# Attention visits taken two units at a time from the sixteenth unit on, and VectorE steps placed on other hooks

## The chip, the cores and the metric

The kernel runs on one core of a Trainium2 chip. The metric is the device time of one execution in microseconds (us). TensorE (PE) multiplies, VectorE (DVE) and ScalarE (ACT) read its results out of PSUM, GpSimd (POOL) works between tiles in SBUF, and SyncE (SP) issues nearly all DMAs, in order.

## The reference

A decayed attention without softmax for 4 batches, 8 heads, 576 positions and head width 64, then two feed-forward layers on the 2304 tokens of width 512, all in float32:

```python
scores = scale * np.matmul(q, k.transpose(0, 1, 3, 2))
Dmat = np.where(rel >= 0, gamma[:, None, None] ** rel[None, :, :], 0.0)
x = np.matmul(scores * Dmat, v)                  # heads side by side: 2304 x 512
h = np.maximum(np.maximum(x @ w1, x @ w2), x @ w3) @ w_out      # 512 -> 768 -> 512
g = h @ w_gate                                                  # 512 -> 1536
out = (g * (1.0 / (1.0 + np.exp(-g))) * (h @ w_val)) @ w_out2   # 1536 -> 512
```

## The kernel before, in words

The program order on every engine is written out by hand, so each engine does its instructions in the order in which the code calls them. Only buffers and data make it wait.

**Attention.** Two heads (a pair `pr`) of one half `h` of a batch make a unit: 32 units, each with 288 positions in three chunks of 96. A visit to unit n is four short runs of matmuls: `a_value(n)` (the part from the running states, L285, and the part from the weighted scores, L289, into `o_ps`), `a_state(n + 1)` (L264, into `m_ps`) and `a_score(n + 1)` (L248, into `s`). ACT copies `o_ps` into `xh` (L292), and DVE makes the remainder `xl` (L294), a chain of small state updates `st` (L274) and the weighted scores `pT` (L250). Later in the visit `a_prep(n + 2)` prepares a unit: POOL scales `ks`, and DVE does two transposes and a product (L233, L234, L235; "the transposes" below).

**Slices.** Between the short runs stand slices of the first feed-forward layer (`f_slice`): 12 matmuls of 288 columns (L358) into one of two buffers `ps`. The result is read by ACT for the first of three weights (L362) and by DVE for the other two (`hmax`, L364). The queue `fq` holds them in the order weight by weight, two halves each, so that of six slices in a row two end on ACT and four on DVE. A slice can begin only when the reader of the slice two before it is done. From unit 16 on a visit holds five slices.

**Early steps.** From unit 16 on each call of `share` also takes one or two steps of `early_steps`, which turns 28 weights of the later layers from doubled words into float32 (`f32_steps`): a load of 512 KB issued two weights ahead, two ACT copies (L115, L121), three DVE operations (L123 and L124 as one step, L126), and a store of 256 KB (L462). Nine such steps fall in a visit. SP also issues in that part the loads of `k` and `v` of a later pair (`a_load`, L167) and its eight transposed pieces `qk` (`t_load`, L188), the former in odd visits and the latter in even ones.

**Middle.** The product with `w_out` runs in six stretches `hx` of 384 tokens (L743). After each of the four result blocks `e` of a stretch, `h_split` makes the high and low parts of the next input (ACT L545; POOL or, for two of six, DVE L546), and some steps of `x_first` or `x_second` prepare the sums of the last layer's Strassen-like scheme (ACT L660, DVE L662 and subtractions of 768 columns).

**Last layers.** 36 groups, each of seven products of six matmuls (L817) into `g1`, `g2`, `g3`, with `out2` (L794, read by DVE L799 or ACT L797) between them. `hook()` is called ten times in a group; it takes steps of `w_steps` (operands of the next block, L602 and L628 to L635) or, in the last three groups before the final twelve, steps of `x_last` by the table `XPLAN` (splits L662, subtractions L699). The groups before the final twelve are numbered j = 0 to 23. The first hook stands just ahead of the second product, whose result DVE takes up as `u` (L833); the product two later on `g2` may start only when that is read. The last hook stands at a group's end.

Of the kernel before, what the change touches and what calls it, by code (L numbers as in the profile page):

```python
# [23 lines left out]
P = 128  # L24
# [44 lines left out]
def retention_moe(ctx, tc, consts, q, k, v, w1, w2, w3, w_out, w_gate, w_val, w_out2, out):  # L69
# [15 lines left out]
    psa_cm = tc.tile_pool(name="ps_att", bufs=1, space=PSUM)  # L85
    psa = psa_cm.__enter__()

    cst_a = att.tile([P, O_G], F32, name="cst_a", tag="cst_a", bufs=1)
    cst_g = att.tile([P, NCONST - O_G], F32, name="cst_g", tag="cst_g", bufs=1)
    ident = cst_a[0:CK, O_ID:O_KS]  # L90
# [50 lines left out]


    PT = 12
    units = [(b, h, pr) for b in range(B) for pr in range(NP) for h in range(2)]
    NU = len(units)
    U = {}
# [61 lines left out]
    def a_prep(n):  # L208

        if n >= NU:  # L210
            return
        bind(n)
        b, h, pr = units[n]
        u = U[n]
        nk = NC - h
        u["ks"] = att.tile([CK, NC, 2, D], F32, name="ks", tag="ks", bufs=3)
        sc = ks_t[:, pr].unsqueeze(1).unsqueeze(3).to_broadcast([CK, nk, 2, D])
        pool.tensor_tensor(u["ks"][:, 0:nk], u["k"][:, 0:nk], sc, ALU.mult)  # L218
        kq = att.tile([P, 2, C], F32, name="kq", tag="kq", bufs=3)
        kt, qg = kq[:, 0], kq[:, 1].rearrange("p (c m) -> p c m", c=NC)  # L220
        g = g_t[:, pr].unsqueeze(1).to_broadcast([P, NC, CK])
        if n < PT:
            tp = psa.tile([P, 2, 512], F32, name="tp", tag="tp")
            for c in range(NC):
                pe.transpose(tp[:, 0, c * CK:(c + 1) * CK], u["k"][:, c].rearrange("p h d -> p (h d)"), ident)
            for c in range(NC):
                for e in range(2):
                    pe.matmul(tp[64 * e:64 * e + 64, 1, c * CK:(c + 1) * CK], u["q"][:, c, e],  # L228
                              dia[pr][:, e], start=True, stop=True)
# [24 lines left out]
    def a_state(n):  # L254

        if n >= NU:
            return
        b, h, pr = units[n]
        u = U[n]
        nk = NC - h  # L260
        m = psa.tile([P, NC, D], F32, name="m_ps", tag="m_ps")
        for c in range(nk):
            for e in range(2):
                pe.matmul(m[64 * e:64 * e + 64, c], u["ks"][:, c, e], u["v"][:, c, e], start=True, stop=True)  # L264
        if h == 0:
            st = states[(b, pr)] = att.tile([P, 2 * NC, D], F32, name="st", tag="st", bufs=3)
        else:
            st = states.pop((b, pr))
        for c in range(nk):
            g = h * NC + c  # L270
            if g == 0:
                act.activation(st[:, 1], m[:, c], ACTF.Copy)
            else:
                dve.scalar_tensor_tensor(st[:, g + 1], st[:, g], e_t[:, pr:pr + 1], m[:, c], ALU.mult, ALU.add)  # L274
        u["st"] = st

    def a_value(n):
# [15 lines left out]
        xs[(2 * b + h, pr)] = (xh, xl)  # L293
        return lambda: dve.tensor_tensor(xl, o, f(xh), ALU.subtract)  # L294


    w_in = {}
    win_units = [(fi, wi) for fi in range(F1) for wi in range(3)]
# [71 lines left out]
    def f_some(n):  # L370
        for _ in range(n):
            if fq:
                f_slice(*fq.pop(0))
# [8 lines left out]
    def visit(n, slices, convs):  # L382
        plan = list(conv_plan(convs))
        done = 0

        def share(j):
            nonlocal done
            upto = len(plan) * (j + 1) // (slices + 1)
# [4 lines left out]
            if n >= 16:  # L393
                for _ in range(1 if j % 2 else 2):
                    next(early, None)

        low = a_value(n)
        if slices:
            share(0)
        if n % 2:  # L400
            a_load(n // 2 + 3)
        else:
            t_load(n // 2 + 2)
        if n % (2 * NP) == 2 * NP - 1:
            fq.extend((n // NP - 1 + h, *w) for w in win_units for h in range(2))
        a_state(n + 1)
        low()
        a_score(n + 1)
        for j in range(slices + 1):
            if j == min(2, slices - 1) or not slices:  # L410
                a_prep(n + 2)
            if j or not slices:
                share(j)
            if j < slices:
                f_some(1)

    EARLY = [(fi, wi) for fi in range(F2) for wi in range(3) if wi < 2 or fi < 3 or fi == F2 - 1]
# [74 lines left out]
    a_state(0)  # L492
    a_prep(1)
    spin(1)
    for n in range(NU):
        if n < NP - 1:
            tables(n + 1)
        if 2 <= n < 6:
            win_load(n - 2)
        if n == 5:  # L500
            win_phase(0, 0)
            win_phase(0, 1)
        if n == 9:
            sp.dma_start(out=cst_g, in_=consts[:, O_G:NCONST])
        visit(n, *((0, 0) if n < 5 else (0, 1) if n < 8 else (4, 2) if n < 13 else (4, 3) if n < 14 else (6, 2) if n < 16 else (5, 0)))
# [164 lines left out]
    def x_second(b, r):  # L670

        t1 = raw("t12")
        dve.tensor_tensor(t1, r["B12"], r["B11"], ALU.subtract)
        yield
        t3 = r["B12"]
        dve.tensor_tensor(t3, r["B22"], t3, ALU.subtract)
        yield
        yield from x_split(b, "T1", t1)
        dve.tensor_tensor(t1, r["B22"], t1, ALU.subtract)
        yield  # L680
        yield from x_split(b, "T3", t3)
# [47 lines left out]
    for hx in range(NHX):  # L729
        b, half = divmod(hx, 2)  # L730
        if half == 0:
            r = {}
            if b < NBK - 1:
                x_open(b)
        for e in range(KD):
            ps = ps_mm.tile([P, 512], F32, name="ps2", tag="mm")
            n = 0
            for fi in range(F1):
                wh, wl = wo[fi]
                hh, hl = hsp[(hx, fi)]  # L740
# [20 lines left out]
        for _ in xsteps:  # L761
            pass
        xsteps = (x_second if half else x_first)(b, r) if b < NBK - 1 else iter(())
    for _ in steps:
        pass
    hw_cm.__exit__(None, None, None)
# [36 lines left out]
    def group(fi, b, hook, lastg=False):  # L803
# [75 lines left out]
        if fi % GRP == GRP - 1:  # L879
# [5 lines left out]
    XPLAN = {(0, 3): 1, (0, 5): 1, (0, 6): 1, (0, 7): 1, (0, 9): 1, (0, 10): 1,  # L885
             (1, 1): 1, (1, 2): 1, (1, 3): 1, (1, 4): 1, (1, 5): 1, (1, 7): 1, (1, 9): 1,
             (2, 1): 1, (2, 2): 1, (2, 4): 1, (2, 5): 1, (2, 7): 1}
    steps = iter(())
    for j, (fi, b) in enumerate(seq):
        if j == 0:  # L890
# [12 lines left out]

        def hook():
            beat[0] += 1
            if j < len(seq) - 3:
                for _ in range(pace):
                    next(steps, None)
            else:
                for _ in range(XPLAN.get((j + 3 - len(seq), beat[0]), 0)):  # L910
                    next(xsteps)

        group(fi, b, hook)
    for _ in xsteps:
# [35 lines left out]
```

## Time and profile before

| | |
|---|---|
| time, median of 3 runs | 830.73 us (830.68 to 832.44) |
| the profiled execution's own time | 830.89 us |
| its span, first to last instruction | 829.1 us |
| granted TensorE clock | 1.00, the 2.4 GHz level |
| PE busy | 816.9 us, 99% of the span |
| DVE / ACT / POOL busy | 566.3 / 315.7 / 209.7 us |

A busy time counts overlapping matmuls once, and the span is 1.8 us shorter than the execution's time. An idle time given with an instruction is counted from the end of the instruction before it on that engine.

### The profile page before, as it was taken

How to read it: one execution, taken by the hardware profiler on the slowest of the kernel's cores; microseconds unless marked ns; L12 is line 12 of the kernel's file. 1: busy time of each engine (PE TensorE's matmuls, PEld its weight loads, DVE VectorE, ACT ScalarE, POOL GpSimd, SP SyncE). 2: the span in 40 equal slices, each digit the busy share in tenths (PEclk: the TensorE clock that was granted, in tenths of full speed). 3: DMA queues.
4: the chain of work that ended last, by engine and by line, in shares of the span. 5: the costliest groups of instructions: out<-in, count | busy, mean ns of one | idle time of the engine just before them, and what ended most of it. 6: DMA issues, size and time to landing. Idle time of an engine off the chain costs nothing.

```text
span 829.1 us, 15469 instructions
## 1 busy us (share of the span) xinstructions
PE 816.9 (99%) x5933; PEld 762.7 (92%) x5933; DVE 566.3 (68%) x1007; ACT 315.7 (38%) x633; POOL 209.7 (25%) x194
## 2 busy tenths in 40 slices
PE   9999999999999999999999999999999999999998
PEld 6799999899989999999999999999999899999996
DVE  2678857787764354477387799888889875455554
ACT  3554523324321223555354544344444332332220
POOL 4243420000000002343032233323332233322331
PEclk9999999999999999999999999999999999999999
DMA  9999849999981233866334334443422016665532
GB/s 178 236 217 214 175 113 252 238 250 245 252 231 70 80 100 93 247 178 187 137 124 152 141 140 165 165 146 134 165 77 70 20 51 242 217 227 214 191 104 76
DMA packets 162921, 135.08 MB, mean 163 GB/s; under 512 B 101024, under 2 KB 137632, under 8 KB 162848
## 3 DMA queue, kind: packets, MB, share of 16 engines
q1 hardware_dynamic: 161488, 133.69, 56.0%
q8 instruction: 46, 0.75, 0.4%
q10 hardware_dynamic: 1360, 0.41, 0.2%
q14 instruction: 27, 0.22, 0.1%
HBM read 89.77 MB, written 44.30 MB: 162 GB/s over the span
## 4 chain that ended last, share of the span: by engine, by line
PE 67%; issue 14%; DVE 7%; POOL 6%; DMA 2%; ACT 2%; SPq 1%; POOLq 0%; ACTq 0%; DVEq 0%
PE ps L358 25%; PE g L817 17%; PE ps L794 11%; PE ps L743 6%; POOL gl L865 3%; POOL p L838 2%; PE s L248 2%; PE o_ps L289 2%; PE o_ps L285 2%; DMA w<-in_moe_w_val_dram 1%; PE m_ps L264 1%; SPq L188 1%; PE tp L228 1%; DMA kn<-in_k_dram 1%; PE psz L380 1%
## 5 line engine op out<-in xcount | busy, mean ns | idle before, releaser
L358 PE MATMUL ps<-xl,wh 128*128 128x288 f32 x576 | 173.1, 300 | 3.4 <-DVE hmax L364 2.8
L358 PE MATMUL ps<-xh,wh 128*128 128x288 f32 x576 | 169.7, 295 | 0.0
L358 PE MATMUL ps<-xh,wlo 128*128 128x288 f32 x576 | 169.6, 294 | 0.0
L865 POOL TENSOR_TENSOR gl<-p,gh 128x384 fp32r<-128x384 f32 x72 | 85.5, 1205 | 290.1 <-ACT gh L864 290.1
L794 PE MATMUL ps<-wp,gh 128*128 128x512 f32 (+1 forms) x436 | 135.4, 392 | 0.8 <-DVE acc L799 0.7
L358 PEld LDWEIGHTS ps<-xl,wh 128*128 128x128 f32 x576 | 108.0, 188 | 7.6 <-DVE hmax L364 4.0
L358 PEld LDWEIGHTS ps<-xh,wh 128*128 128x128 f32 x576 | 108.1, 188 | 0.0
L358 PEld LDWEIGHTS ps<-xh,wlo 128*128 128x128 f32 x576 | 108.1, 188 | 0.0
L794 PEld LDWEIGHTS ps<-wp,gh 128*128 128x128 f32 x436 | 80.7, 188 | 15.1 <-DVE acc L799 1.8
L364 DVE TENSOR_TENSOR hmax<-ps,hmax 128x288 f32<-128x288 f32 x96 | 43.5, 455 | 69.0 <-PE ps L358 61.1
L794 PE MATMUL ps<-wp,gl 128*128 128x512 f32 (+1 forms) x218 | 85.6, 393 | 0.0
L799 DVE TENSOR_TENSOR acc<-ps,acc 128x512 f32<-128x512 f32 (+1 forms) x91 | 61.9, 683 | 29.5 <-PE ps L794 28.3
L817 PE MATMUL g<-xhB,wa 128*128 128x384 f32 x288 | 73.4, 336 | 0.0
L817 PE MATMUL g<-xhT,wc 128*128 128x384 f32 x288 | 73.2, 335 | 0.0
L546 POOL TENSOR_TENSOR hl<-hf,hh 128x384 fp32r<-128x384 f32 x26 | 30.0, 1164 | 129.3 <-DMA h_d<-hmax 77.4
L864 ACT ACTIVATE gh<-p 128x384 fp32r<-128x384 f32 x72 | 37.8, 525 | 61.0 <-DVE p L868 53.5
L218 POOL TENSOR_TENSOR ks<-kn,cst_a 96x384 f32<-96x384 f32 (+1 forms) x32 | 26.4, 826 | 126.1 <-PE m_ps L264 107.8
L853 ACT ACTIVATE sb<-u 128x384 f32<-128x384 f32 x36 | 18.9, 525 | 100.0 <-DVE u L851 100.0
L817 PEld LDWEIGHTS g<-xhB,wa 128*128 128x128 f32 x288 | 52.1, 188 | 0.0
L817 PEld LDWEIGHTS g<-xhT,wc 128*128 128x128 f32 x288 | 52.0, 188 | 0.0
L362 ACT ACTIVATE hmax<-ps 128x288 f32<-128x288 f32 x48 | 19.7, 410 | 84.1 <-PE ps L358 83.8
L794 PEld LDWEIGHTS ps<-wp,gl 128*128 128x128 f32 x218 | 40.9, 188 | 9.0
(120 smaller groups left out, 1694.1 us busy)
## 6 DMA issues: line engine op xcount, KB each, us to landing
w<-in_moe_w_out_dram SPq DMA_DIRECT2D x18, 512.0 KB, 4.1
w<-l_d SPq DMA_DIRECT2D x28, 256.0 KB, 3.0
h_d<-hmax SPq DMA_DIRECT2D x48, 144.0 KB, 3.3
w<-in_moe_w_dram SPq DMA_DIRECT2D x12, 512.0 KB, 6.6
w<-in_moe_w_gate_dram SPq DMA_DIRECT2D x12, 512.0 KB, 5.9
w<-in_moe_w_val_dram SPq DMA_DIRECT2D x12, 512.0 KB, 5.9
vn<-in_v_dram SPq DMA_DIRECT2D x16, 288.0 KB, 7.9
out_dram<-acc SPq DMA_DIRECT2D x17, 256.0 KB, 2.0
```

The lines of the kernel that those rows point to most:

```text
L218: pool.tensor_tensor(u["ks"][:, 0:nk], u["k"][:, 0:nk], sc, ALU.mult)
L358: pe.matmul(ps, l[:, ksl], r, start=n == 0, stop=n == 3 * KD - 1)
L362: act.activation(mx[hb], ps, ACTF.Copy)
L364: dve.tensor_tensor(mx[hb], ps, mx[hb], ALU.max)
L546: (dve if fi in (3, 5) and hx else pool).tensor_tensor(hl, hf, f(hh), ALU.subtract)
L743: pe.matmul(ps[:, 0:HT], l[:, es], rr, start=n == 0, stop=n == 3 * F1 - 1)
L794: pe.matmul(ps[:, cs], l[:, sl], r[:, cs], start=n == 0, stop=n == 3 * GRP - 1)
L799: dve.tensor_tensor(a[:, cs], ps[:, cs], a[:, cs], ALU.add)
L817: pe.matmul(ps, l[:, ks], r[:, kc], start=first and n == 0, stop=n == 5, skip_group_check=True)
L853: act.activation(sb, u2, ACTF.Sigmoid)
L864: act.activation(gh[half], t, ACTF.Copy)
L865: pool.tensor_tensor(gl[half], t, f(gh[half]), ALU.subtract)
```

## The change

**Double visits.** Units 0 to 15 keep their visits. At the end of unit 15 the PSUM pool is exchanged (`swap_banks`) for one with two tiles: `s4` with four banks, which holds the scores of two units and, in the free columns of its first two banks, their state products; and `o2` with two banks. From then on `visit_pair(j)` handles units 2j and 2j + 1 together: all four runs are of double length, and ten slices follow. The state chain and the two score weightings are called one by one ahead of the first three slices, and the two preparations ahead of the fourth and the sixth. `a_load(j + 3)` and `t_load(j + 3)` stand one behind the other near the start of the pair. `share` is called 11 times in a pair and takes 17 early steps there, against 18 in two visits. `kq` has four buffers, `ks` and `st` two.

**Middle.** In `x_second` the split of T4 moves ahead of those of T2 and B22. In the stretch `hx = 4` the blocks take 4, 4, 2 and 0 steps instead of 4, 4, 3 and 3, and the rest follows in `hx = 5`.

**Last layers.** `XPLAN` is given anew for j = 21 to 23, and three hooks take no step (`CALM`): the last of j = 2, the first of j = 3, the first of j = 20. The steps there move to later hooks.

```diff
+    def swap_banks():
+        nonlocal psa_cm, psa
+        psa_cm.__exit__(None, None, None)
+        psa_cm = tc.tile_pool(name="ps_pair", bufs=1, space=PSUM, reuse_waits="tile")
+        psa = psa_cm.__enter__()
...
+    PP = 16
...
-        kq = att.tile([P, 2, C], F32, name="kq", tag="kq", bufs=3)
+        kq = att.tile([P, 2, C], F32, name="kq", tag="kq", bufs=4)
...
+    def pair_value(j):
+        o = psa.tile([P, 2, 512], F32, name="o_ps", tag="o2")
+        us = [U.pop(2 * j + h) for h in range(2)]
+        for h, u in enumerate(us):
+            for c in range(1 - h, NC):
+                for e in range(2):
+                    hd = slice(64 * e, 64 * e + 64)
+                    pe.matmul(o[hd, h, c * CK:(c + 1) * CK], u["st"][hd, h * NC + c], u["qg"][hd, c],
+                              start=c == 1 - h, stop=False, skip_group_check=True)
+        for h, u in enumerate(us):
+            for c in range(NC):
+                for e in range(2):
+                    pe.matmul(o[64 * e:64 * e + 64, h, c * CK:(c + 1) * CK], u["v"][:, c, e], u["pT"][:, e, c],
+                              start=False, stop=True, skip_group_check=True)
...
+    def pair_next(j):
...
+        s = psa.tile([P, 4, 512], F32, name="s", tag="s4")
+        m = [s[:, h, C + c * D:C + (c + 1) * D] for h in range(2) for c in range(NC - h)]
...
+        def chain_states():
+            act.activation(st[:, 1], m[0], ACTF.Copy)
+            for g in range(1, 2 * NC - 1):
+                dve.scalar_tensor_tensor(st[:, g + 1], st[:, g], e_t[:, pr:pr + 1], m[g], ALU.mult, ALU.add)
...
+        return [chain_states, lambda: weigh(0), lambda: weigh(1)]
...
+    def visit_pair(j, slices, convs):
+
+        share = sharing(min(slices, 8 if convs else slices), convs, j >= 8)
+        pair_value(j)
+        share(0)
+        a_load(j + 3)
+        t_load(j + 3)
+        if j % NP == NP - 1:
+            fq.extend((2 * (j // NP) + h, *w) for w in win_units for h in range(2))
+        late = pair_next(j + 1)
+        for x in range(slices + 1):
+            if late:
+                late.pop(0)()
+            if x in (3, 5):
+                a_prep(2 * j + 4 + (x == 5))
+            if x:
+                share(x)
+            if x < slices:
+                f_some(1)
...
-    for n in range(NU):
+    for n in range(PP):
...
+    for j in range(PP // 2, NU // 2):
+        visit_pair(j, 10, 0)
...
+        yield from x_split(b, "T4", t3)
         yield from x_split(b, "T2", t1)
         yield from x_split(b, "B22", r["B22"])
-        yield from x_split(b, "T4", t3)
...
-            for _ in range(4 if e < 2 else 3):
+            for _ in range((4, 4, 2, 0)[e] if hx == NHX - 2 else 2 if hx == NHX - 1 else 4 if e < 2 else 3):
                 next(xsteps, None)
...
+    XPLAN = {0: (3, 4, 5, 6, 7, 9), 1: (1, 2, 5, 6, 7, 9), 2: (2, 3, 4, 5, 6, 7)}
+    CALM = ((2, 10), (3, 1), (len(seq) - 4, 1))
...
+            elif (j, beat[0]) not in CALM:
                 for _ in range(pace):
                     next(steps, None)
```

On PE, in the attention part, two visits before read as follows (five slices of L358 stand between the first four rows and the last four; an x6 is six pairs of passes in the trace):

```order
L285 MATMUL o_ps<-kq,st 64x96 x6
L289 MATMUL o_ps<-pT,vn 64x96 x6
L264 MATMUL m_ps<-vn,ks 64x64 x6
L248 MATMUL s<-kq 96x96 x6
...
L285 MATMUL o_ps<-kq,st 64x96 x4
L289 MATMUL o_ps<-pT,vn 64x96 x6
L264 MATMUL m_ps<-vn,ks 64x64 x4
L248 MATMUL s<-kq 96x96 x6
```

One pair of the changed kernel, with the L-numbers of its own file:

```order
L311 MATMUL o_ps<-kq,st 64x96 x10
L316 MATMUL o_ps<-pT,vn 64x96 x12
L339 MATMUL s<-vn,ks 64x64 x10
L346 MATMUL s<-kq 96x96 x12
```

The same small matmuls now stand in four runs instead of eight, and the slices of both visits follow them in one row of ten.

On DVE, one visit before, from the state chain to the last `hmax`:

```order
L274 SCALAR_TENSOR_TENSOR st<-st,cst_a,m_ps 128x64 x2
L294 TENSOR_TENSOR xl<-o_ps,xh 128x288
L250 TENSOR_TENSOR pT<-s,dm_88 96x576
L364 TENSOR_TENSOR hmax<-ps,hmax 128x288
L123 TENSOR_SCALAR wz<-wz 128x512
L124 SCALAR_TENSOR_TENSOR wz<-w_2267,wz 128x512
L364 TENSOR_TENSOR hmax<-ps,hmax 128x288
L233 STREAM_TRANSPOSE kq<-qk 128x288
L234 STREAM_TRANSPOSE qt<-qk 128x288
L235 TENSOR_TENSOR kq<-qt,cst_g 128x288
L126 ISA wl<-wz,wl 128x1024
L364 TENSOR_TENSOR hmax<-ps,hmax 128x288 x2
```

And a stretch of pair 8 of the changed kernel, from the end of its third slice to that of its fifth:

```order
L430 TENSOR_TENSOR hmax<-ps,hmax 128x288
L240 STREAM_TRANSPOSE kq<-qk 128x288
L241 STREAM_TRANSPOSE qt<-qk 128x288
L242 TENSOR_TENSOR kq<-qt,cst_g 128x288
L430 TENSOR_TENSOR hmax<-ps,hmax 128x288
L129 TENSOR_SCALAR wz<-wz 128x512
L130 SCALAR_TENSOR_TENSOR wz<-w_1857,wz 128x512
L132 ISA wl<-wz,wl 128x1024
L430 TENSOR_TENSOR hmax<-ps,hmax 128x288
```

The transposes and a full early step stand between different `hmax` there, and the chain and both `pT` stand ahead of this stretch.

On DVE, at the seam between the groups j = 2 and j = 3 of the last layers, before:

```order
L872 TENSOR_TENSOR p_5594<-sa,p_5594 128x384
L602 TENSOR_TENSOR wc<-wz,wc 128x512
L833 TENSOR_TENSOR u_5701<-g_5680,p_5688 128x384
L602 TENSOR_TENSOR wd<-wz,wd 128x512
L602 TENSOR_TENSOR wp<-w_5598,wp 128x512
L845 TENSOR_TENSOR p_5710<-g_5680,p_5710 128x384
```

and in the changed kernel:

```order
L979 TENSOR_TENSOR p_5566<-sa,p_5566 128x384
L940 TENSOR_TENSOR u_5669<-g_5651,p_5659 128x384
L707 TENSOR_TENSOR wc<-wz,wc 128x512
L707 TENSOR_TENSOR wd<-wz,wd 128x512
L952 TENSOR_TENSOR p_5678<-g_5651,p_5678 128x384
```

The low part of `wc` moves from ahead of `u` to behind it.

## Rows read from the trace of the kernel before

**Rows 1.** The page's head and busy times.
```profile
span 829.1 us, 15469 instructions
...
PE 816.9 (99%) x5933; PEld 762.7 (92%) x5933; DVE 566.3 (68%) x1007; ACT 315.7 (38%) x633; POOL 209.7 (25%) x194
```

**Rows 2.** Waits of PE: total us, times, longest us.
```profile
PE ps L358 <- DVE hmax L364: 2.8, 4, 1.2
PE g L817 <- DVE u L833: 1.8, 3, 0.7
...
PE ps L794 <- DVE acc L799: 0.7, 2, 0.4
PE ps L358 <- ACT hmax L362: 0.5, 1, 0.5
```

**Rows 3.** Timeline of PE, visits 21 and 22: start us, length us, engine, line.
```profile
172.59 0.29 PE L358 MATMUL ps<-xh,wh 128*128 128x288 f32 x1
172.81 0.71 PE L285 MATMUL o_ps<-kq,st 64*64 64x96 f32 x12
...
174.00 0.52 PE L264 MATMUL m_ps<-vn,ks 96*64 96x64 f32 x12
174.44 0.75 PE L248 MATMUL s<-kq 64*96 64x96 f32 x12
...
175.36 0.29 PE L358 MATMUL ps<-xh,wlo 128*128 128x288 f32 x1
175.49 0.29 PE L358 MATMUL ps<-xh,wh 128*128 128x288 f32 x1
...
183.27 0.55 PE L285 MATMUL o_ps<-kq,st 64*64 64x96 f32 x8
...
184.29 0.40 PE L264 MATMUL m_ps<-vn,ks 96*64 96x64 f32 x8
```

**Rows 4.** Timeline of PE around one late slice of visit 19.
```profile
156.13 0.29 PE L358 MATMUL ps<-xh,wh 128*128 128x288 f32 x1
156.90 0.40 PE L358 MATMUL ps<-xl,wh 128*128 128x288 f32 x1 [0.47 <-DVE hmax L364]
157.14 0.30 PE L358 MATMUL ps<-xh,wlo 128*128 128x288 f32 x1
```

**Rows 5.** Timeline of DVE in the same visit.
```profile
156.40 0.81 DVE L364 TENSOR_TENSOR hmax<-ps,hmax 128x288 f32<-128x288 f32 x2
157.13 0.47 DVE L233 STREAM_TRANSPOSE kq<-qk 128x288 f32<-128x288 f32 x1
...
158.36 0.42 DVE L123 TENSOR_SCALAR wz<-wz 128x512 uint32<-128x512 uint32 x1
...
160.24 0.45 DVE L364 TENSOR_TENSOR hmax<-ps,hmax 128x288 f32<-128x288 f32 x1
```

**Rows 6.** Timeline of SP's queue: loads of v and of qk.
```profile
196.16 2.07 SPq L167 DMA_DIRECT2D vn<-in_v_dram  x1
...
206.06 4.25 SPq L188 DMA_DIRECT2D qk<-in_k_dram  x4
210.36 2.38 SPq L188 DMA_DIRECT2D qk<-in_q_dram  x4
```

**Rows 7.** Waits of ACT: total us, times, longest us.
```profile
ACT wz L115 <- DMA w<-in_moe_w_gate_dram: 5.4, 4, 1.8
```

**Rows 8.** Timeline of PE in the middle part, stretch hx = 5.
```profile
396.50 0.45 PE L743 MATMUL ps<-hl,woh 128*128 128x384 f32 x1 [0.25 <-DVE hl L546]
...
397.41 0.45 PE L743 MATMUL ps<-hl,woh 128*128 128x384 f32 x1
```

**Rows 9.** Timeline of ACT just before it.
```profile
394.61 0.83 ACT L660 ACTIVATE xhB<-B 128x768 fp32r<-128x768 f32 x1
```

**Rows 10.** Timeline of DVE at the ends of groups 2 and 21.
```profile
433.33 1.50 DVE L602 TENSOR_TENSOR wc<-wz,wc 128x512 fp32r<-128x512 f32 x1
...
652.86 1.77 DVE L699 TENSOR_TENSOR w<-w,w 128x768 f32<-128x768 f32 x1
```

More of the change, by code (lines that the diff above doesn't have):

```diff
@@ L215, in a_prep @@
         nk = NC - h
-        u["ks"] = att.tile([CK, NC, 2, D], F32, name="ks", tag="ks", bufs=3)
+        u["ks"] = att.tile([CK, NC, 2, D], F32, name="ks", tag="ks", bufs=2)
         sc = ks_t[:, pr].unsqueeze(1).unsqueeze(3).to_broadcast([CK, nk, 2, D])
         pool.tensor_tensor(u["ks"][:, 0:nk], u["k"][:, 0:nk], sc, ALU.mult)
-        kq = att.tile([P, 2, C], F32, name="kq", tag="kq", bufs=3)
+        kq = att.tile([P, 2, C], F32, name="kq", tag="kq", bufs=4)
         kt, qg = kq[:, 0], kq[:, 1].rearrange("p (c m) -> p c m", c=NC)
@@ L265, in a_state @@
         if h == 0:
-            st = states[(b, pr)] = att.tile([P, 2 * NC, D], F32, name="st", tag="st", bufs=3)
+            st = states[(b, pr)] = att.tile([P, 2 * NC, D], F32, name="st", tag="st", bufs=2)
         else:
@@ L294, in a_value @@
         return lambda: dve.tensor_tensor(xl, o, f(xh), ALU.subtract)
+    def pair_value(j):
[12 more added lines that the diff above has]
+                              start=False, stop=True, skip_group_check=True)
+        b, _, pr = units[2 * j]
+        low = []
+        for h in range(2):
+            xh, xl = [ffn.tile([P, C], F32R, name=f"x{x}", tag=f"x{x}{pr}", bufs=4) for x in "hl"]
+            act.activation(xh, o[:, h, 0:C], ACTF.Copy)
+            xs[(2 * b + h, pr)] = (xh, xl)
+            low.append((xh, xl, h))
+        for xh, xl, h in low:
+            dve.tensor_tensor(xl, o[:, h, 0:C], f(xh), ALU.subtract)
@@ new lines, in pair_next, with weigh @@
+    def pair_next(j):
+        if j >= NU // 2:
+            return []
+        b, _, pr = units[2 * j]
+        us = [U[2 * j + h] for h in range(2)]
+        s = psa.tile([P, 4, 512], F32, name="s", tag="s4")
+        m = [s[:, h, C + c * D:C + (c + 1) * D] for h in range(2) for c in range(NC - h)]
+        for h, u in enumerate(us):
+            for c in range(NC - h):
+                for e in range(2):
+                    pe.matmul(m[h * NC + c][64 * e:64 * e + 64], u["ks"][:, c, e], u["v"][:, c, e],
+                              start=True, stop=True)
+        for h, u in enumerate(us):
+            for c in range(NC):
+                cs = slice(c * CK, (c + 1) * CK)
+                for e in range(2):
+                    hd = slice(64 * e, 64 * e + 64)
+                    pe.matmul(s[0:CK, 2 * e + h, cs], u["kt"][hd, cs], u["qg"][hd, c], start=True, stop=True)
+        st = att.tile([P, 2 * NC, D], F32, name="st", tag="st", bufs=2)
+        def chain_states():
+            act.activation(st[:, 1], m[0], ACTF.Copy)
+            for g in range(1, 2 * NC - 1):
+                dve.scalar_tensor_tensor(st[:, g + 1], st[:, g], e_t[:, pr:pr + 1], m[g], ALU.mult, ALU.add)
+        def weigh(h):
+            pT = us[h]["pT"] = att.tile([CK, 2, NC, CK], F32, name="pT", tag="pT")
+            dve.tensor_tensor(pT, s[0:CK].rearrange("p (e h) m -> p h e m", h=2)[:, h, :, 0:C].rearrange("p e (c m) -> p e c m", c=NC),
+                              d_t[pr].unsqueeze(2).to_broadcast([CK, 2, NC, CK]), ALU.mult)
+        for u in us:
+            u["st"] = st
+        return [chain_states, lambda: weigh(0), lambda: weigh(1)]
@@ L380, in spin, with sharing @@
             pe.matmul(ps, zero[:, 0:P], zero, start=True, stop=True)
-    def visit(n, slices, convs):
+    def sharing(spread, convs, joins):
         plan = list(conv_plan(convs))
@@ L387, in share @@
             nonlocal done
-            upto = len(plan) * (j + 1) // (slices + 1)
+            upto = len(plan) * (j + 1) // (spread + 1)
             for step in plan[done:upto]:
@@ L392, in share, with visit @@
             done = upto
-            if n >= 16:
+            if joins:
                 for _ in range(1 if j % 2 else 2):
                     next(early, None)
+        return share
+    def visit(n, slices, convs):
+        share = sharing(slices, convs, False)
         low = a_value(n)
@@ L401, in visit @@
             a_load(n // 2 + 3)
-        else:
+        if n % 2 == 0:
             t_load(n // 2 + 2)
+        elif n == PP - 1:
+            t_load(PP // 2 + 2)
         if n % (2 * NP) == 2 * NP - 1:
             fq.extend((n // NP - 1 + h, *w) for w in win_units for h in range(2))
-        a_state(n + 1)
+        if n + 1 < PP:
+            a_state(n + 1)
         low()
-        a_score(n + 1)
+        if n + 1 < PP:
+            a_score(n + 1)
+            late = []
+        else:
+            swap_banks()
+            late = pair_next(PP // 2)
+        ahead = [n + 2] if n < PP - 2 else [PP, PP + 1] if n < PP - 1 else [PP + 2, PP + 3]
         for j in range(slices + 1):
+            if late:
+                late.pop(0)()
             if j == min(2, slices - 1) or not slices:
-                a_prep(n + 2)
+                a_prep(ahead.pop(0))
+            if j == 4 and ahead:
+                a_prep(ahead.pop(0))
             if j or not slices:
@@ L414, in visit @@
             if j < slices:
+                f_some(1)
[9 more added lines that the diff above has]
+        for x in range(slices + 1):
+            if late:
+                late.pop(0)()
+            if x in (3, 5):
[3 more added lines that the diff above has]
+            if x < slices:
                 f_some(1)
@@ L504, in retention_moe @@
             sp.dma_start(out=cst_g, in_=consts[:, O_G:NCONST])
-        visit(n, *((0, 0) if n < 5 else (0, 1) if n < 8 else (4, 2) if n < 13 else (4, 3) if n < 14 else (6, 2) if n < 16 else (5, 0)))
+        visit(n, *((0, 0) if n < 5 else (0, 1) if n < 8 else (4, 2) if n < 13 else (4, 3) if n < 14 else (6, 2)))
         if n < 8:
@@ L760, in retention_moe @@
                     next(steps, None)
-        for _ in xsteps:
-            pass
-        xsteps = (x_second if half else x_first)(b, r) if b < NBK - 1 else iter(())
+        if hx != NHX - 2:
+            for _ in xsteps:
+                pass
+        if b < NBK - 1:
+            xsteps = (x_second if half else x_first)(b, r)
     for _ in steps:
@@ L884, in retention_moe @@
     beat = [0]
-    XPLAN = {(0, 3): 1, (0, 5): 1, (0, 6): 1, (0, 7): 1, (0, 9): 1, (0, 10): 1,
-             (1, 1): 1, (1, 2): 1, (1, 3): 1, (1, 4): 1, (1, 5): 1, (1, 7): 1, (1, 9): 1,
-             (2, 1): 1, (2, 2): 1, (2, 4): 1, (2, 5): 1, (2, 7): 1}
+    XPLAN = {0: (3, 4, 5, 6, 7, 9), 1: (1, 2, 5, 6, 7, 9), 2: (2, 3, 4, 5, 6, 7)}
+    CALM = ((2, 10), (3, 1), (len(seq) - 4, 1))
     steps = iter(())
@@ L905, in hook @@
             beat[0] += 1
-            if j < len(seq) - 3:
+            if j >= len(seq) - 3:
+                if beat[0] in XPLAN[j + 3 - len(seq)]:
+                    next(xsteps)
+            elif (j, beat[0]) not in CALM:
                 for _ in range(pace):
                     next(steps, None)
-            else:
-                for _ in range(XPLAN.get((j + 3 - len(seq), beat[0]), 0)):
-                    next(xsteps)
         group(fi, b, hook)
```

## The prediction

> **What bounds the kernel now.** I read the page first: PE is busy for 816.9 of 829.1 us, while DVE is at 68% and ACT at 38% [rows 1]. So the time is PE's row of matmuls with its gaps, and whatever another engine gains counts only where PE waits for it. The list of PE's waits says where that is, and it is short: five waits for a reader of a slice, three for `u`, two for `acc`; the timeline adds one for a low part in the middle [rows 2, 8]. But an idle time understates a wait. At the late slice of visit 19 PE starts at 156.90 after 156.13, where the usual step is 0.13, so 0.64 us are lost and not 0.47; and the second matmul comes 0.24 later and not 0.13, which is 0.11 more [rows 3, 4]. I therefore add 0.28 to each idle time. Third, I read PE's timeline across a visit, because short runs of small matmuls cost PE time that no list of waits shows.
>
> **Seams between forms.** From the last matmul of one slice (172.59) to the second of the next (175.36) there are 2.77 us. Two of the usual steps are 0.26 (175.36 to 175.49 is 0.13), which leaves 2.51 for the visit itself. What do its matmuls cost where they follow their own kind? Visit 22 has two pairs fewer in L285 and in L264: 0.55 against 0.71 and 0.40 against 0.52 [rows 3]. That is 0.08 for a pair of L285 and 0.06 for one of L264. L289 and L248 move 96 columns like L285, so I give them 0.08. Six pairs of each are 6 x 0.30 = 1.80. The remaining 0.7 is paid by the visit for changing the form of its matmuls, however many there are of each. With rounded lengths I take 0.66. A pair has one set of runs where two visits have two, and units 16 to 31 make eight pairs, so 8 x 0.66 = 5.3 us go. The bounds are nothing (if the second unit's half of each run pays again for its other PSUM bank) and 8 x 0.7 = 5.6. I take the upper part, since from L289 to L264 the output tile changes too, and L264 begins at 174.00 with the usual run behind it.
>
> **Waits in the attention part.** Of the five slice waits of [rows 2] the longest, 1.2, is at 104 us, in visit 14, which keeps its form. The other four are 2.8 - 1.2 + 0.5 = 2.1 us idle, with 4 x 0.28 some 3.2. What makes them is DVE's order. In visit 19 the three transposes and a whole early step stand between two `hmax`: DVE goes from 157.13 to 160.24, 3.1 us, while a slice takes 12 x 0.13 = 1.6 [rows 3, 5]. In a pair the order puts them between different ones. By starts, the transposes take 1.23 (157.13 to 158.36), the early step 1.88 (to 160.24), an `hmax` about 0.37 (156.40 to 157.13 for two) [rows 5]. So `hmax` follows `hmax` at 1.60 or 2.25, and three slices of 4.8 us meet 1.60 + 2.25 + 1.60 = 5.45 of DVE work. The slip of 0.65 is within what a buffer allows: a reader may start 1.6 - 0.45 = 1.1 late before PE stands still. A wait arises only where DVE comes into this stretch more than 0.45 late, from the chain and two `pT` ahead of it. The total of DVE's work is unchanged, so I don't take all of the 3.2. The bounds are 3.2 gained and nothing gained; I take 1.9, with 1.3 coming back in some pairs. ACT's and POOL's parts keep their count; a `ks` is made two runs earlier than its use, and costs nothing under ten slices of 1.6 us.
>
> **SP.** `kn`, `vn` and eight `qk` now stand in one row: 4.25 + 2.38 for `qk` and up to 2.07 for `vn` are 8.7 us, and with the shorter `kn` (0.5 is my estimate) some 9.2, against 6.6 at a time before [rows 6]. Behind them wait the weights of the early steps, for which ACT already waits up to 1.8 us [rows 7]. Each is asked for two weights ahead, and four early steps make one weight: at 17 steps in a pair of some 20 us that is 2 x 4 x 20 / 17, some 9 us of notice. I count nothing for it, as 17 early steps in a pair instead of 18 also ask for less; its price otherwise is a rival below.
>
> **Tail.** Pair 14 has ten slices where visit 30 found only two left, so 28 instead of 31 remain behind the attention part. The sum of slices is the same: nothing.
>
> **Middle.** At 396.50 PE waits 0.25 for a low part that DVE makes from `hh`; with 0.28 that is 0.5. The next low part is late too: 397.41 is 0.91 behind, where three steps of 384 columns (0.17 each, by 0.13 for 288) and 0.11 make 0.62, so 0.3 and again 0.11 for what follows. I count 0.9. `hh` stood on ACT behind the split of B22, 0.83 [rows 8, 9]. That split goes to the next stretch. `hh` then comes 0.8 earlier, more than either step is late: 0.9 gained, at worst nothing.
>
> **Last layers.** `u` was late three times: 1.8 idle, with 3 x 0.28 some 2.6. One of the waits for `acc` (0.4 + 0.28, in group 22, behind a subtraction) makes 3.3 [rows 2]. In each of the three a long DVE step lies ahead of `u`: `wc` with 1.50 at the last hook of group 2, a subtraction of 1.77 at that of group 21, and two steps at the first hook of group 20 [rows 10]. All three are moved behind `u`, where DVE's next result is due two products and two `out2` later. But in groups 21 and 22 a subtraction now stands on the fifth hook, ahead of the reading of the first `out2`. A third `out2` may start only after that: one product and two `out2` later, some 3.8 us, against 2 x 0.55 + 1.77 + 0.68 = 3.5 on DVE. That is close, so I leave 0.5 for it: 2.8 gained, between 1.3 (two such waits at 0.7, and 0.6 for a late `u`) and 3.3.
>
> **Sum.** 5.3 + 1.9 + 0.9 + 2.8 = 10.9 from the execution's own 830.9: 820.0. The median lies 0.16 lower, so 819.8.
>
> **Rivals.**
> (a) *The chain waits for the scores.* State products and scores now share a tile and two banks, where `m_ps` was a tile apart. If the chain starts only when all scores are written, it starts two L248 runs later: one is 0.75 long with its last matmul's end [rows 3], so some 1.3 us per pair, just ahead of the stretch in which DVE has 0.45 to spare. At most 0.8 of it reaches PE in each of eight pairs, 6 us; with half of that 823, within 820 to 826. Against it speaks that DVE has two `xl` to do meanwhile. The Trainium skill, page "PSUM — Partial Sum Buffer", section "PSUM bank collisions raise a hardware error", says that two engines must not touch one bank and quadrant at the same time and that software should guard by bank; by that rule this rival is the rule and not the exception, and the time would be its 823. No run before shows it, since there no tile was shared so.
> (b) *The weights come late.* This is the one on the other side. SP's row is 2.6 us longer. If each of the five pairs with loads (8 to 12) passes this on to ACT, from there to DVE's early step and so to `hmax`, PE loses up to 2.6 in each: 13 us, 833. From 2.5 us per pair it decides the sign at 832.4. Half of it is 826. Before, waits of 1.8 for a weight cost PE only 0.6 to 0.7 at a time [rows 4, 7], which speaks against the full price.
> (c) *The seams stay* (a second bank costs what a second form does): 825.1.
> (d) *Every wait goes:* 830.9 - 5.6 - 3.2 - 0.9 - 3.3 = 817.9, by the median 817.7.
> (e) *The last layers only move their waits:* 822.6.
>
> **Chances.** The sum as it stands, between 818 and 822: 0.58. (d): 0.10. (a): 0.10, between 820 and 826. (b) in part, 822 to 832: 0.12, in full: 0.03. (c): 0.04. (e): 0.03. The range from 817.5 to 825.5 leaves out most of (b) and some of (a) and (d), less than 2 in 10. About 0.2%, 1.7 us, is what a measurement of this kernel can tell from no change; slower by more than that needs the full (b): 0.03. Within it lies only the upper end of the partial (b): 0.02. Faster: 0.95.
>
> **What would show it.** Right: a pair's runs from the last matmul of a slice to the second of the next take about 4.3 us (twice 2.77, less 0.28 for the shorter runs of every second visit, 0.26 and 0.66); PE's waits for `hmax` in the attention part sum to less than before; the wait for `hl` and those for `u` are gone. Wrong: waits of ACT's L121 (L115 before) for weights of over 3 us in each pair with PE idle behind them; a chain whose first operation stands behind the last score matmul; new waits for `acc` in groups 21 to 23.

## The result and the profile after

The changed kernel takes 821.73 us (median of 4 runs, 821.22 to 822.78); beside it the kernel before took 831.36 (4 runs), a ratio of 0.9889 with an interval of 0.9876 to 0.9903. The forecast was 819.8, in a range of 817.5 to 825.5. The gain was forecast as 10.9 us and is 9.6; the rest of the distance from 819.8 to 821.73 is the kernel before, which took 831.36 here and 830.73 when the forecast was made. The profiled execution took 821.22 at a span of 819.4.

First the page of the changed kernel, head and busy times, which answer to [rows 1]:

```profile
span 819.4 us, 15460 instructions
...
PE 808.4 (99%) x5925; PEld 760.6 (93%) x5933; DVE 561.5 (69%) x1007; ACT 315.1 (38%) x633; POOL 209.3 (26%) x194
```

PE is as full as before, at 99%, and DVE, ACT and POOL run as many instructions as before. PE's busy time is 8.5 lower, but 2.6 of this lie in the first 40 us (34.72 against 37.33), where the records of eight matmuls are missing in this trace (x5925 against x5933). So the page doesn't tell where the gain comes from; that is read from the first matmul of the middle part and of the last layers. Before (timeline of PE):

```profile
331.89 0.34 PE L743 MATMUL ps<-hl,woh 128*128 128x384 f32 x1
...
407.94 0.34 PE L817 MATMUL g<-xlB,wa 128*128 128x384 f32 x1
```

After, in the same view:

```profile
324.81 0.34 PE L848 MATMUL ps<-hl,woh 128*128 128x384 f32 x1
...
400.54 0.34 PE L924 MATMUL g<-xlB,wa 128*128 128x384 f32 x1
```

The part up to the last slice is 331.89 - 324.81 = 7.1 shorter (forecast 5.3 + 1.9 = 7.2). The middle goes from 76.05 to 75.73, 0.3 (forecast 0.9). The rest of the span's 9.7 is 2.3, in the last layers (forecast 2.8).

PE's waits in the changed kernel, as in [rows 2] (total, times, longest):

```profile
PE ps L424 <- DVE hmax L430: 1.2, 1, 1.2
...
PE ps L424 <- ACT hmax L428: 0.5, 1, 0.5
PE g L924 <- ACT p L934: 0.4, 1, 0.4
PE ps L901 <- DVE acc L906: 0.3, 1, 0.3
```

The wait of 1.2 is that of visit 14, which is no pair. The waits for `u` and for `hl` are gone from the list, and a new one for a copy `p` of `g1` has come. One pair on PE's timeline, to be read against [rows 3]:

```profile
160.37 0.29 PE L424 MATMUL ps<-xh,wh 128*128 128x288 f32 x1
160.59 1.04 PE L311 MATMUL o_ps<-kq,st 64*64 64x96 f32 x20
161.56 1.21 PE L316 MATMUL o_ps<-pT,vn 96*64 96x96 f32 x24
162.60 0.75 PE L339 MATMUL s<-vn,ks 96*64 96x64 f32 x20
163.28 1.26 PE L346 MATMUL s<-kq 64*96 64x96 f32 x24
164.47 0.40 PE L424 MATMUL ps<-xl,wh 128*128 128x288 f32 x1
164.71 0.29 PE L424 MATMUL ps<-xh,wlo 128*128 128x288 f32 x1
```

From the last matmul of a slice to the second of the next there are 164.71 - 160.37 = 4.34 us; 4.3 was forecast.

### The profile page after: what moved, and what is told of

Read it like the earlier page. It is cut to its first block, busy times and chain, and to the rows that moved or that the text cites. A ratio compares the mean times of both kernels' runs of the same rounds, so it can differ in the third digit from the quotient of the medians.

```text
span 819.4 us, 15460 instructions
## 1 busy us (share of the span) xinstructions
PE 808.4 (99%) x5925; PEld 760.6 (93%) x5933; DVE 561.5 (69%) x1007; ACT 315.1 (38%) x633; POOL 209.3 (26%) x194
## 4 chain that ended last, share of the span: by engine, by line
PE 90%; DVE 5%; DMA 2%; issue 1%; ACT 1%; POOL 0%; SPq 0%; ACTq 0%; DVEq 0%
PE g L924 31%; PE ps L424 27%; PE ps L901 18%; PE ps L848 6%; DMA l_d<-wl 1%; PE o_ps L296 1%; PE s L346 1%; PE o_ps L292 1%; PE s L255 1%; PE o_ps L316 1%; PE o_ps L311 1%; PE tp L235 1%; PE m_ps L271 1%; DMA vn<-in_v_dram 1%; PE s L339 0%
## 5 line engine op out<-in xcount | busy, mean ns | idle before, releaser
L225 POOL TENSOR_TENSOR ks<-kn,cst_a 96x384 f32<-96x384 f32 (+1 forms) x32 | 24.6, 777 | 118.4 <-PE s L339 86.5
L952 DVE TENSOR_TENSOR p<-g,p 128x384 f32<-128x384 f32 x36 | 19.9, 554 | 43.3 <-PE g L924 34.2
```

Of the source, the lines that this page charges most:

```text
L952: dve.tensor_tensor(p5, g2, p5, ALU.add)
```

## The experiments

**Are the terms independent?** Two kernels carry one half of the change each: `e1_pairs_only` the double visits, `e2_rest_only` the edits of the middle and the last layers.

> Double attention visits alone; the middle and the last layers take their steps as before. Theory (three independent terms): the attention part up to the last slice is 7.1 us shorter as in the changed kernel (8 x 0.66 at the seams, the rest from waits), the middle and the last layers as before, so 830.9 - 7.1 = 823.8, ratio about 0.991. Rival (the terms lean on each other, since the shifted attention part moves the waits of the last layers): the sum of this run's gain and that of the run without double visits differs from the whole gain of 9.6 by more than 1 us.

> Single attention visits throughout; only the edits of the middle and the last layers. Theory: the middle gains 0.3 and the last layers 2.3 as in the changed kernel, so 830.9 - 2.6 = 828.3, ratio about 0.997, and a new wait of about 0.65 us at the second product on g1 of group 21 stands here too. Rival: those waits depend on what the attention part left behind, and this run gains under 1.5 or over 3.7.

The double visits alone take 824.35 us (ratio 0.9919, 0.9904 to 0.9934), the rest alone 829.16 (0.9978, 0.9965 to 0.9991), beside 831.38 for the kernel before. The gains of 7.0 and 2.2 add to 9.2, against 9.6 for both. The difference of 0.4 is less than the intervals can tell (about 1.2 either way for each run), so no dependence shows. On the timeline the middle begins at 324.89 in the first; in the second the last layers, from 408.60 to the end of its span of 827.5, take 418.9 as in the changed kernel. The new wait for `p` stands there too, so it belongs to the hooks and not to the attention part:

```profile
641.24 0.44 PE L819 MATMUL g<-xlB,wa 128*128 128x384 f32 x1 [0.36 <-ACT p L829]
```

**What is a seam?** `e3_by_unit` keeps the pairs and their rows of ten slices, and lets the small matmuls go unit by unit:

```diff
             for c in range(1 - h, NC):
                 ...
-        for h, u in enumerate(us):
             for c in range(NC):          # value part; the same in pair_next
```

> The changed kernel, but inside a pair the small matmuls go unit by unit again: values of the first unit, its weighted scores, then those of the second; and state products and scores likewise. The same matmuls, seven changes between small forms in a pair instead of three; the slices still stand in one row of ten. Theory (each change of form is paid, some 0.12 us by the steps that exceed the usual ones): 4 x 0.12 = 0.5 more in each of 8 pairs, a pair's stretch of 4.34 becomes 4.8, and the time 821.7 + 3.6 = 825.3. Rival (only leaving the slices and coming back to them is paid, 0.66 at a time): 4.34 stays and the time is 821.7.

It took 826.47 (ratio 0.9943, 0.9929 to 0.9956), 4.7 more than the changed kernel. The same pair on its timeline:

```profile
162.26 0.29 PE L422 MATMUL ps<-xh,wh 128*128 128x288 f32 x1
162.48 0.55 PE L311 MATMUL o_ps<-kq,st 64*64 64x96 f32 x8
162.96 0.72 PE L315 MATMUL o_ps<-pT,vn 96*64 96x96 f32 x12
163.60 0.71 PE L311 MATMUL o_ps<-kq,st 64*64 64x96 f32 x12
164.24 0.72 PE L315 MATMUL o_ps<-pT,vn 96*64 96x96 f32 x12
...
167.22 0.29 PE L422 MATMUL ps<-xh,wlo 128*128 128x288 f32 x1
```

L338 and L344 follow in two runs each in the same way. The stretch is 167.22 - 162.26 = 4.96 and not 4.34: four more changes of form cost 0.62, some 0.155 each, and eight pairs make 5.0 of it (the last has fewer runs). Two visits before take 2.77 + 2.49 - 0.26 = 5.00 for the same matmuls. But the two visits have six changes between small forms and leave the slices twice, where `e3_by_unit` has seven changes and leaves them once. So one leaving and return costs 0.04 more than a change, some 0.2 by these starts, and the 0.66 that a pair saves is three changes (0.47) and one leaving and return (0.2). The expectation's rival, that only the leaving is paid, is out; the theory's 0.12 for a change was a little low.

**Are the weights late, and does it matter?** `e6_loads_apart` moves `t_load(j + 3)` from the start of the pair to its sixth slice.

> The changed kernel with the eight transposed loads of a pair asked for ahead of its sixth slice instead of right behind the loads of k and v. In the changed kernel ACT waits 18.9 us in 6 times for a weight of the early steps, longest 6.8, and DVE comes late to the slices of pair 10 (0.21 and 0.66 lost on TensorE). Theory (the contiguous loads hold up the weights): ACT's longest wait falls under 3 us, the waits of 0.21 and 0.66 go, the time falls by 0.9. Rival (the weights are late for another cause, such as the total traffic): ACT's waits stay about 19 us in sum and TensorE's stay.

ACT's waits for the weights (total, times, longest), in the changed kernel:

```profile
ACT wz L121 <- DMA w<-in_moe_w_val_dram: 18.9, 6, 6.8
```

and with the loads apart:

```profile
ACT wz L121 <- DMA w<-in_moe_w_val_dram: 7.6, 4, 2.3
```

The first half of the theory holds: the contiguous loads hold the weights up, and apart from them the longest wait falls to 2.3. The second half falls: the time is 821.79 (0.9890, 0.9874 to 0.9907), the same, and the waits of 0.21 and 0.66 in pair 10 stand as they did. Late weights were not their cause. In other executions of the same code they do add to the first of the two: in `e12_after_again` and `e8_mid_last`, both below, ACT's wait ahead of pair 10 was 7.15 and 7.32 instead of 6.78, DVE's chain in the pair began 0.3 and 0.4 later, and the slice lost 0.50 and 0.65 instead of 0.21.

**Does the spread on DVE matter?** `e7_bunched` calls the chain and both weightings at once (`while late` for `if late`) and both preparations ahead of the fourth slice.

> The changed kernel, but with its VectorE work in bunches: the state chain and both weightings right behind each other ahead of the first slice, both preparations ahead of the fourth. Same instructions, same seams on TensorE. Theory (the spread is what keeps hmax on time): between the hmax of the third and the fourth slice there are 2.46 + 1.88 + 0.37 = 4.7 us of DVE, against 1.6 for a slice and 1.1 allowed, so up to 2.0 are lost in each pair with an early step there; with half of the pairs hit the time is 821.7 + 8 = 830. Rival (only DVE's total counts, and the two buffers carry the rest): within 1 us of 821.7.

It took 827.70 (0.9958, 0.9943 to 0.9974): 6.0 more than the changed kernel, with the same seams. PE's waits for `hmax` rise from 1.2 in one to this:

```profile
PE ps L424 <- DVE hmax L430: 5.1, 7, 1.4
```

The instructions are the same, so that is their order, on DVE above all (POOL's `ks` of the second preparation moves along); 6.0 is below the 8 estimated. With `e6_loads_apart` it says that the order makes most of the waits. `e10_steps_late` then gave the first five calls of `share` one early step each and the last six two:

```diff
-                for _ in range(1 if j % 2 else 2):
+                for _ in range(1 if j < 5 else 2):
```

> The changed kernel with the 17 early steps of a pair shared out 1, 1, 1, 1, 1 ahead of the first slices and 2 at each of the six later calls, instead of 2 and 1 in turn. Theory (what is left of the waits for hmax comes from DVE's work ahead of the second to sixth slice, early steps above all, not from late weights): the waits of pairs 10 and 13 in the changed kernel (0.2 to 0.7 each, 1.1 to 2.1 in sum by the runs so far) go, the attention part falls from 283.0 to 284.1 to about 282, the time to some 820.7. Rival (the weights come late and the steps are late wherever they stand): the waits move to the later slices, nothing is gained.

It took 822.27 (0.9895, 0.9881 to 0.9908). The waits of pairs 10 and 13 went, but another came, 0.91 idle at 157.30, in pair 9. The theory on the place was right for pairs 10 and 13 and the repair wrong: the sixth call now puts a whole early step behind the second transposes of the pair, between one `hmax` and the next (DVE's timeline):

```profile
153.30 0.46 DVE L430 TENSOR_TENSOR hmax<-ps,hmax 128x288 f32<-128x288 f32 x1 [1.37 <-DMA qk<-in_q_dram]
...
156.18 0.69 DVE L132 CUSTOM_DVE_ANT_0 wl<-wz,wl 128x1024 uint16<-128x1024 uint16 x1
156.79 0.81 DVE L430 TENSOR_TENSOR hmax<-ps,hmax 128x288 f32<-128x288 f32 x2
```

156.79 - 153.30 = 3.5 us, the bunch of [rows 5] again. DVE had not come late to it: it stood idle for 1.37 until the slice that the first `hmax` reads was written (on PE's timeline its last matmul ends at 153.21; the DMA that the row names is not what it waited for). In the changed kernel an early step fills that gap.

**More pairs.** `e4_from14` begins the pairs at unit 14 (`PP = 14`, the first pair with 12 slices and 4 weight conversions).

> The changed kernel with double visits from unit 14 on: nine pairs, the first with twelve slices. Theory: one more seam of 0.66 goes, and the wait of 1.3 in visit 14, which comes from the same order on DVE, goes in part: 821.7 - 0.7 to 821.7 - 2.0. Rival: the weights of the first layer that are converted there on POOL, ACT and DVE hold up the slices of that pair; then the wait stays or grows and nothing is gained.

It took 823.76 (0.9913, 0.9898 to 0.9928), 2.0 more than the changed kernel. The rival held, at another place than the slices: the state products of the first pair stand for `ks` of unit 17, which POOL makes behind the low part of a weight (PE, then POOL):

```profile
100.12 0.45 PE L339 MATMUL s<-vn,ks 96*64 96x64 f32 x8 [2.56 <-POOL ks L225]
...
97.69 1.81 POOL L142 TENSOR_TENSOR wlo<-wl,wh 128x512 fp32r<-128x512 f32 x1 [2.58 <-ACT wh L140]
99.46 0.61 POOL L225 TENSOR_TENSOR ks<-kn,cst_a 96x256 f32<-96x256 f32 x1
```

The stop has a second price. The granted clock, 1.00 until then, stood at 0.50, the 1.2 GHz level, from 100.59 to 104.00:

```profile
100.51 2.20 PE L346 MATMUL s<-kq 64*96 64x96 f32 x24
...
100.60:104.00 3.40, 3.40 (x29) 3.23 (x30) 2.00 (x7) 1.45 (x4) 2.04 (x2) 0.50 1.25 198
```

The scores took 2.20 where they took 1.26 in the pair above, and the slice's first matmuls followed at 0.24 instead of 0.13: some 1.5 us by these starts, beside 2.8 for the stop itself. The mean clock of all five executions is 0.996 to 0.998, where the changed kernel has 0.999 and 1.000, so the kept trace is not alone in it. Without the fall the time would be some 822.3 (an estimate), still no less than the changed kernel's.

`e9_from14_early_ks` prepares unit 17 earlier in visit 13 (`j == 2` for `j == 4`).

> Double visits from unit 14 on, and the preparation of unit 17 already ahead of the third slice of visit 13 instead of behind its fourth, so that ks on POOL does not stand behind the low part of a weight. Theory (the 2.77 lost at the state products of the first pair were all of that run's loss): they go, and the time is that run's 823.8 less 2.8 to 3.0, about 820.9, just under the changed kernel's 821.7. Rival: two preparations side by side make DVE late for hmax in visit 13, 1 us or more comes back there and nothing is gained over 821.7.

The wait for `ks` went, the clock stayed at 1.00, and 822.69 us (0.9898, 0.9880 to 0.9916) is 1.1 less than 823.76, but still 1.0 above the changed kernel. The rival's outcome came at another place than it said: visit 13 has no late slice, but in the first pair three slices wait 0.52, 1.49 and 0.51 for their readers, ACT once and DVE twice. Beginning the pairs earlier gained nothing in either form.

**The two terms that fell short.** `e8_mid_last` repairs the middle and the last layers:

```diff
-            for _ in range((4, 4, 2, 0)[e] if hx == NHX - 2
+            for _ in range((4, 4, 1, 1)[e] if hx == NHX - 2
...
-                for _ in range(pace):
+                for _ in range(4 if (j, beat[0]) == (len(seq) - 4, 2) else pace):
```

> The changed kernel with two repairs. Middle: in the stretch hx = 4 the blocks take 4, 4, 1, 1 steps, so that the low part of T4 on DVE stands behind the two low parts hl instead of ahead of them. Theory (hl was held up there by DVE's 0.96 for that part, not by hh): the 0.24 and 0.12 with 2 x 0.11 at TensorE go, some 0.5. Last layers: the two steps left out at the first hook of group 20 are made up for at its second hook. Theory (the low part of wp on DVE made the product p, then gh on ACT, then the copy of g1 late): the wait of 0.54 + 0.11 at the second product on g1 of group 21 goes. Both: 821.7 - 1.1 = 820.6. Rival: hh and the copy of g1 are late by themselves, and both waits stay.

Both waits went. By its starts the middle takes 75.41 (75.73 in the changed kernel) and the last layers with the end 417.95 (418.9): 1.3 together, where 1.1 was expected. The last layers gave more than the wait for `p`, since the third `out2` of group 21 comes on time too.

```profile
325.84 0.34 PE L848 MATMUL ps<-hl,woh 128*128 128x384 f32 x1
...
401.25 0.34 PE L924 MATMUL g<-xlB,wa 128*128 128x384 f32 x1
```

The time is 820.92 (0.9878, 0.9862 to 0.9894). The attention part, whose code is untouched, took 1.0 more in this profiled execution, all of it at late slices of the pairs 10 and 13. `e12_after_again` ran the changed kernel once more:

> The changed kernel again, beside the two others on the same chip. It should stand within 0.5 us of 821.7; the attention part should show how far the waits of pairs 10 and 13 differ between executions of one program.

821.59 (0.9882, 0.9869 to 0.9896); its middle begins at 325.13, where it was 324.81, with waits of 0.50 and 0.66 in pair 10 instead of 0.21 and 0.66. So `e8_mid_last` is lower by 0.7 to 0.8 by medians, which its interval does not separate from the changed kernel; its shorter parts are read from the trace. `e11_all` adds the late early steps and a later preparation in visit 14 (`3 if n == PP - 2 else 2`).

> The repairs of the middle and the last layers, the early steps shared out late, and in visit 14 the first of the two preparations one slice later. Theory (the parts add up): 1.2 for the middle and the last layers, some 1.0 for the early steps, and the wait of 1.3 with 0.3 in visit 14 goes in part: 821.7 - 2.2 to 821.7 - 3.8. Rival: the preparation of unit 17 comes later by as much as that of unit 16, and the state products or scores of the first pair wait for it; then the gain stays under 2.2.

The parts did not add up: 820.98 (0.9878, 0.9864 to 0.9893), a gain of some 0.7 where 2.2 to 3.8 was expected. The wait of 0.91 in pair 9 that the late early steps made in `e10_steps_late` stands here too, and visit 14 waits 0.18 and 0.51 instead of 1.2. The trace also shows how a late weight does reach PE, where the reader of a slice stands behind it on ACT:

```profile
200.62 0.66 ACT L121 ACTIVATE wz<-w 128x512 f32<-128x512 f32 x1 [2.67 <-DMA w<-in_moe_w_gate_dram]
...
201.75 0.38 ACT L428 ACTIVATE hmax<-ps 128x288 f32<-128x288 f32 x1
```

PE's next slice begins at 202.19, after 1.51 us idle. The profiled execution, 822.45, was the longest of the four, by 1.26; whether the others had this wait is not known.

## Why the prediction was right, point by point

**Seams: right.** 8 x 0.66 = 5.3 was forecast; 4.34 against 5.00 is 0.66 in a pair. That the second unit's bank would not pay again was chosen, not known. Now it shows: L311 with 20 takes 1.04, with 12 0.71, with 8 0.55 (the last two in `e3_by_unit`), so about 0.08 for each pair of matmuls also where the run passes into the second bank. Rival (c) is out.

**Waits in the attention part: right in size, and for most of them in cause.** 7.1 less the seams' 5.3 is 1.8; 1.9 was forecast. Counted by starts, the late slices from visit 16 on cost 3.5 before and 1.7 after, where the forecast had 3.2 and 1.3. Most of what is left is in pair 10. Its first late slice begins at 167.95, right behind the `hmax` that frees its buffer, and that stands behind the chain, where the prediction put it. The second is of another kind. DVE, ACT and PE:

```profile
166.31 1.22 DVE L352 SCALAR_TENSOR_TENSOR st<-st,cst_a,s 128x64 f32<-128x64 f32 x4
167.45 0.45 DVE L430 TENSOR_TENSOR hmax<-ps,hmax 128x288 f32<-128x288 f32 x1
...
172.78 0.45 DVE L430 TENSOR_TENSOR hmax<-ps,hmax 128x288 f32<-128x288 f32 x1
...
173.02 0.41 ACT L428 ACTIVATE hmax<-ps 128x288 f32<-128x288 f32 x1 [3.44 <-PE ps L424]
...
172.70 0.29 PE L424 MATMUL ps<-xh,wh 128*128 128x288 f32 x1
173.49 0.40 PE L424 MATMUL ps<-xl,wh 128*128 128x288 f32 x1 [0.50 <-ACT hmax L428]
```

DVE's `hmax` is late there too (173.23, where PE could have begun at 172.83), but PE begins 0.06 behind the end of ACT's read at 173.43, as the list of waits says. That read is of the slice just before: the new slice takes the buffer of its predecessor and not that of the slice two before. `e7_bunched` has this twice, and the second time DVE's `hmax` for the other buffer begins only after PE has gone on:

```profile
239.92 0.40 PE L424 MATMUL ps<-xl,wh 128*128 128x288 f32 x1 [0.50 <-ACT hmax L428]
240.19 0.45 DVE L430 TENSOR_TENSOR hmax<-ps,hmax 128x288 f32<-128x288 f32 x1
```

The wait of 0.5 for ACT in [rows 2] is of the same kind (PE begins at 160.84, ACT's read ended at 160.79), so the prediction put one of its four waits down to DVE's order where PE waited for ACT. Why the program takes the other buffer at these places no run here shows; in `e10_steps_late`, where DVE has less to do ahead of this slice, it doesn't.

**SP: right in the sum, not in the reason.** Nothing was counted because 17 early steps ask for less than 18; the loads do hold the weights up all the same (longest wait of ACT 6.8, before 1.8), which is the first half of rival (b). In the changed kernel's trace ACT and DVE had time for it, and taking most of it away changed nothing. The second half, the way on to PE, is there as well: 0.3 and 0.4 more at one slice of pair 10 in `e12_after_again` and `e8_mid_last`, where the weight was 0.4 and 0.5 later still, and 1.5 in one place of `e11_all`. It stayed far from the 2.5 per pair that would have decided the sign.

**Rival (a): its mechanism is there, its price is not.** The chain's first operation waits for the last score (ACT's timeline):

```profile
164.59 0.22 ACT L350 ACTIVATE st<-s 128x64 f32<-128x64 f32 x1 [0.95 <-PE s L346]
```

The state products were written by about 163.3, when the scores began. In pair 10 DVE was busy with an early step until 166.31, so nothing was lost by it. In pairs 8 and 12 DVE did stand idle for the chain, 0.95 and 0.46, and no slice was late there. The Trainium skill, page "PSUM — Partial Sum Buffer", section "PSUM bank collisions raise a hardware error", asks for a guard by bank. By the kernel's code the copy reads the first bank, which gets its last score in the first half of L346, by some 163.96 (twelve take 0.68 in `e3_by_unit`; an estimate). It began at 164.59, behind all 24. So the trace shows more waiting than the page's rule asks for, a wait for the whole tile, and still the 823 did not come. A layout without the shared tile was not tried.

**Middle: the step that failed** is "`hh` then comes 0.8 earlier, more than either step is late: 0.9 gained". `hh` came 387.54 - 324.81 = 62.73 after the start of the middle, where it was 395.35 - 331.89 = 63.46, so 0.73 earlier. But `hl` did not follow. The changed kernel (ACT, DVE, POOL):

```profile
387.54 1.34 ACT L650 ACTIVATE hh<-hf 128x384 fp32r<-128x384 f32 x3
...
387.68 0.96 DVE L767 TENSOR_TENSOR xlT<-B,xhT 128x768 fp32r<-128x768 f32 x1 [1.35 <-ACT xhT L765]
388.55 1.84 DVE L651 TENSOR_TENSOR hl<-hf,hh 128x384 fp32r<-128x384 f32 x2
...
388.54 1.44 POOL L651 TENSOR_TENSOR hl<-hf,hh 128x384 fp32r<-128x384 f32 x1 [4.89 <-ACT hh L650]
```

The low part of T4 had moved ahead along with its split, and DVE was in it until 388.6: the first `hl` began 1.01 behind the start of `hh`, where it had been 0.54 (395.89 - 395.35). 0.3 came instead of 0.9; with that part behind `hl` (`e8_mid_last`) another 0.3.

**Last layers: the mechanism right, one cost missed.** All three waits for `u` went, and the one for `acc` in group 22. The 0.5 set aside for the fifth hook came as about 0.26 (the third `out2` of group 21 begins at 639.38). Not foreseen was the other end of group 20: its steps, put off by the first hook, ran to its end, and the low part of `wp` stood ahead of `acc`, `u` and `p`. The chain from there (DVE, ACT, PE):

```profile
629.85 0.69 DVE L707 TENSOR_TENSOR wp<-w,wp 128x512 fp32r<-128x512 f32 x1 [1.17 <-ACT wp L705]
...
632.24 0.52 ACT L971 ACTIVATE gh<-p 128x384 fp32r<-128x384 f32 x1 [2.42 <-DVE p L975]
632.67 0.47 ACT L934 ACTIVATE p<-g 128x384 f32<-128x384 f32 x1
...
633.19 0.44 PE L924 MATMUL g<-xlB,wa 128*128 128x384 f32 x1 [0.37 <-ACT p L934]
```

ACT's copy of `g1` stands behind `gh`, and PE behind the copy: 0.37 + 0.28 = 0.65. So 2.3 came and not 2.8, and `e8_mid_last` brought 0.9 back, the 0.65 and the 0.26.

## What to carry to other kernels

Short runs of matmuls of different forms are worth merging by form, and the price is read from the start times around them, since no list of waits has it. When a step is moved to free one wait, follow everything that it pulls or pushes along on its engine to the next result that the bound engine needs: both terms that fell short here were such a neighbour. A long wait of an engine off the critical path is no loss until the reader of a busy buffer stands behind it, and that can differ between executions of one program. The name in a list of waits is checked against the end of what it names: where PE begins 0.06 behind a read, that read was it.

## What was not expected of the hardware

A change between two small forms of matmul cost some 0.155 us, on the mean of four, while passing from one PSUM bank to another inside a run cost nothing that shows. Subtractions on DVE and POOL slowed each other when they ran side by side: in the changed kernel two `hl` on DVE took 1.84 together and POOL's 1.44 beside them, where the shortest of POOL's take 1.01. In `e8_mid_last` DVE's first, which is over when POOL has hardly begun, took 0.56, and its second, beside POOL, 1.06:

```profile
389.21 0.56 DVE L651 TENSOR_TENSOR hl<-hf,hh 128x384 fp32r<-128x384 f32 x1 [1.77 <-ACT hh L650]
390.03 1.06 DVE L651 TENSOR_TENSOR hl<-hf,hh 128x384 fp32r<-128x384 f32 x1 [0.27 <-ACT hh L650]
...
389.67 1.01 POOL L651 TENSOR_TENSOR hl<-hf,hh 128x384 fp32r<-128x384 f32 x1 [4.90 <-ACT hh L650]
```

The granted clock fell to half behind one stop of PE of 2.56 us in `e4_from14`, and cost some 1.5 us beyond it. And three profiled executions of the same attention code began the middle at 324.81, 325.13 and 325.84, with 0.21, 0.50 and 0.65 lost at the same slice of pair 10, where ACT had waited 6.78, 7.15 and 7.32 for a weight: a margin this thin is decided by when a DMA lands.
